# Folding the even rows of an fp32 sequence transform on the output side: matmuls of 189, 189 and 378 columns for three of 377

## Chip, cores, metric

One core of one Trainium2 chip; nothing else runs on it. The metric is the device time of one execution in microseconds, median of repeated runs.

## The reference

Shortened:

```python
batch, seq, dim = (8, 3008, 256)              # x
X = np.fft.fft(x, axis=1)                     # the sequence transform
X = np.fft.fft(X, axis=2)                     # the feature transform
attn = X.real
h = attn.reshape(B * S, D) @ w_in             # 24064 x 256 @ 256 x 2048
out = np.maximum(0.01 * h, h) @ w_out         # 2048 x 256
```

Everything is fp32. The kernel does the sequence transform as matmuls against cosine and sine tables, folds the feature transform into `w_in`, and uses a seven-product scheme for `w_out`.

## The kernel before

S = 3008, H = S/2, Q = S/4 = 752. Rows s and S-s, and rows s and H-s, are already added or subtracted on the input side, so that 377 even rows s = 2m (r = 0) and 376 odd ones (r = 1) remain, in three chunks of 128 partitions. A "unit" is one batch and one parity c of the output index k; a unit has two blocks (cosine, sine). The even sum and the odd sum of a block go to two PSUM banks, and their sum and difference are the outputs k and H+k.

```python
KW = [377, 376]                # columns of parity c

def m_order(r):
    m = np.arange(P)[:, None] + P * np.arange(NI)
    return np.where(m < (377, 376)[r], m, -1)

def dft_ps():                  # four banks, shared with cos_ps and sin_ps of up()
    return ps.tile([P, 512], F32, tag="up", bufs=4, name="dft_ps")

def sequence(ps_t, m, z_of, n, c):
    for i in range(NI):        # NI = 3                                  <- line 319
        nc.tensor.matmul(ps_t[0:m, 0 : KW[c]], lhsT=z_of(i), rhs=tabs[n, c][:, i, 0 : KW[c]],
                         start=(i == 0), stop=(i == NI - 1))

def butterfly(t, even_ps, odd_ps, m, c):
    kw, rest = KW[c], UW[c] - KW[c]
    ev = work.tile([P, KC], F32, tag="ev", bufs=2, name="ev")
    nc.scalar.copy(ev[0:m, 0:kw], even_ps[0:m, 0:kw])
    nc.vector.tensor_tensor(t[0:m, 0:kw], ev[0:m, 0:kw], odd_ps[0:m, 0:kw], op=ALU.add)
    nc.vector.tensor_tensor(t[0:m, kw : UW[c]], ev[0:m, 0:rest], odd_ps[0:m, 0:rest], op=ALU.subtract)
```

The rest of the program is a stream of steps. `up` makes hidden values from a finished unit (8 fp32 matmuls of 251 columns, line 386; VectorE adds the Nyquist term and forms g; ScalarE applies the leaky ReLU, line 397), `down` multiplies by `w_out` (7 matmuls of 251 columns, line 449, or 8 in the first two groups of 251 columns, line 429). The transforms of the next unit are emitted between the steps:

```python
def step(at):
    ...                        # up(j, f); three parts per unit, f = 0..7
    if f == 4:
        if part == 0: ...      # fold the rows of the next batch
        elif n > 0:
            dft(units[n + 1], part - 1)()
    ...                        # down of three steps ago

# the start, cut
convert(w0); fold_w_in(0, w0); convert(w2); fold_w_in(2 * WN, w2); spread_wn(0)()
fold_nyquist(); fold_rows(t0, 0); fold_rows(t0, 1); fold_halves(0, t0)
nyquist(0)()                   # the Nyquist column, 8 rows, by the same sequence()
dft(units[0], 0)(); spread(units[0]); dft(units[0], 1)()
o = load_w_out(0); convert(o); some_steps(2); ...
```

A compile-time list scheduler fixes the order of instructions on each engine ("the built order" below); the order in the source is not binding.

## Time and profile before

| | before |
|---|---|
| time, median of 3 | 1966.28 us |
| TensorE busy | 1945.9 us, 99% of the span |
| VectorE, GpSimd, ScalarE busy | 56%, 53%, 24% |
| waits of TensorE in all | 14 us, all before 40 us |

A matmul row of the profile reads: line, engine, operation, output <- inputs, shape, count | busy time, mean ns of one record | idle time before it. Because records overlap, the mean is a latency, not a cost; the cost is read from how far apart the records start. The lines themselves are in the prediction.

### The profile page before, as it was taken

What the parts mean: (1) busy time and instruction counts of PE and PEld (TensorE: products, weight loads), DVE (VectorE), ACT (ScalarE), POOL (GpSimd) and SP (SyncE); (2) the same over time, 40 slices, a digit from 0 to 9 for tenths busy, and PEclk for the clock granted to TensorE, in tenths of its full rate; (3) what the DMA queues carried; (4) which work ended last, traced back from release to release, by engine and by line L of the source; (5) the groups of instructions that cost most, each with busy time, mean ns of one, the idle gap of its engine ahead of it and who ended that gap; (6) DMA issues with size and microseconds to landing.
All of it is one profiled execution on the core that took longest, in us unless ns stands there. A gap on an engine that the chain in (4) does not pass through costs nothing.

```text
span 1964.4 us, 24292 instructions
## 1 busy us (share of the span) xinstructions
PE 1945.9 (99%) x8920; PEld 1687.8 (86%) x8920; DVE 1090.4 (56%) x2075; ACT 462.4 (24%) x526; POOL 1036.1 (53%) x1508
## 2 busy tenths in 40 slices
PE   7999999999999999999999999999999999999999
PEld 3788888888888888888888888888888888888888
DVE  8765455474545655466545654547545474545544
ACT  4422222222222222222222222222222222222221
POOL 0215555565555655556555665556645565555554
PEclk9999999999999999999999999999999999999999
DMA  8120000110001000020000200002000020000000
GB/s 314 41 86 19 11 19 22 35 60 11 19 22 75 19 11 30 11 81 13 22 19 11 83 22 11 19 11 83 22 11 19 11 94 11 16 14 22 11 11 22
DMA packets 25598, 70.99 MB, mean 36 GB/s; under 512 B 4596, under 2 KB 17268, under 8 KB 23432
## 3 DMA queue, kind: packets, MB, share of 16 engines
q1 hardware_dynamic: 23360, 69.43, 9.6%
q8 instruction: 71, 1.16, 0.3%
q14 instruction: 47, 0.39, 0.1%
q10 hardware_dynamic: 2120, 0.02, 0.1%
HBM read 44.72 MB, written 24.71 MB: 35 GB/s over the span
## 4 chain that ended last, share of the span: by engine, by line
PE 98%; DVE 1%; DMA 1%; ACT 0%; SPq 0%; issue 0%; DVEq 0%
PE sum_ps L449 56%; PE cos_ps L386 16%; PE sin_ps L386 16%; PE dft_ps L319 6%; PE sum_ps L429 3%; DMA raw<-in_w_in_dram 1%; PE up_ps L286 0%; DVE xt L189 0%; DVE power L262 0%; DVE win L263 0%; DVE xt L191 0%; DVE xt L200 0%; DVE xt L192 0%; DMA nyq_dram<-nyq 0%; ACT power L250 0%
## 5 line engine op out<-in xcount | busy, mean ns | idle before, releaser
L391 DVE SCALAR_TENSOR_TENSOR cos<-nb,wn,cos_ps 128x251 f32<-128x251 f32 (+1 forms) x768 | 330.6, 472 | 719.5 <-PE cos_ps L386 719.4
L397 ACT ACTIVATE g<-g 128x1004 f32<-128x1004 f32 (+1 forms) x384 | 399.1, 1039 | 1316.2 <-DVE g L396 1308.9
L404 POOL TENSOR_TENSOR s<-g 128x251 f32<-128x251 f32 (+1 forms) x368 | 271.7, 738 | 781.2 <-ACT g L397 781.2
L449 PE MATMUL sum_ps<-s,wt 128*128 128x251 f32 (+1 forms) x2208 | 527.6, 374 | 0.0
L449 PEld LDWEIGHTS sum_ps<-s,wt 128*128 128x128 f32 x2208 | 416.1, 188 | 52.6
L386 PE MATMUL sin_ps<-mix,wf 128*128 128x251 f32 (+1 forms) x1536 | 387.6, 374 | 0.8 <-DVE mix L327 0.8
L386 PE MATMUL cos_ps<-mix,wf 128*128 128x251 f32 (+1 forms) x1536 | 387.9, 374 | 0.0
L449 PE MATMUL sum_ps<-g,wo 128*128 128x251 f32 (+1 forms) x1472 | 372.5, 375 | 0.0
L386 PEld LDWEIGHTS cos_ps<-mix,wf 128*128 128x128 f32 x1536 | 291.2, 190 | 35.8 <-issue 1.0
L386 PEld LDWEIGHTS sin_ps<-mix,wf 128*128 128x128 f32 x1536 | 290.4, 189 | 35.7 <-DVE mix L327 1.2
L449 PEld LDWEIGHTS sum_ps<-g,wo 128*128 128x128 f32 x1472 | 279.6, 190 | 38.7
L395 DVE TENSOR_TENSOR g<-cos,sin_ps 128x502 f32<-128x502 f32 (+1 forms) x384 | 259.9, 677 | 49.9 <-DVE cos L391 9.3
L405 POOL TENSOR_TENSOR s<-s,g 128x251 f32<-128x251 f32 (+1 forms) x368 | 277.7, 755 | 0.0
L407 POOL TENSOR_TENSOR s<-g,s 128x251 f32<-128x251 f32 (+1 forms) x368 | 262.6, 714 | 28.6
L396 DVE TENSOR_TENSOR g<-cos,sin_ps 128x502 f32<-128x502 f32 (+1 forms) x384 | 257.2, 670 | 0.0
L406 POOL TENSOR_TENSOR s<-g 128x251 f32<-128x251 f32 (+1 forms) x368 | 241.6, 657 | 0.0
L449 PE MATMUL sum_ps<-g,wt 128*128 128x251 f32 (+1 forms) x736 | 215.8, 375 | 0.0
L449 PE MATMUL sum_ps<-s,wo 128*128 128x251 f32 (+1 forms) x736 | 215.8, 375 | 0.0
L449 PEld LDWEIGHTS sum_ps<-s,wo 128*128 128x128 f32 x736 | 139.5, 189 | 16.3
L449 PEld LDWEIGHTS sum_ps<-g,wt 128*128 128x128 f32 x736 | 139.8, 190 | 15.8
L319 PE MATMUL dft_ps<-tab,xt 128*128 128x377 f32 (+1 forms) x384 | 126.8, 479 | 1.0 <-DVE xt L199 1.0
L319 PEld LDWEIGHTS dft_ps<-tab,xt 128*128 128x128 f32 x384 | 72.7, 189 | 44.1 <-DVE xt L199 1.7
(46 smaller groups left out, 531.1 us busy)
## 6 DMA issues: line engine op xcount, KB each, us to landing
xt<-in_x_dram SPq DMA_DIRECT2D x16, 1536.0 KB, 9.6
out_dram<-o SPq DMA_DIRECT2D x80, 251.0 KB, 2.3
tab<-in_seq_tab_dram SPq DMA_DIRECT2D x8, 565.5 KB, 11.1
raw<-in_w_in_dram SPq DMA_DIRECT2D x8, 512.0 KB, 5.4
raw<-in_w_out_dram SPq DMA_DIRECT2D x8, 512.0 KB, 4.5
out_dram<-o SPq DMA_DIRECT2D x16, 250.0 KB, 2.4
nb<-nyq_dram SPq DMA_DIRECT2D x8, 376.5 KB
nb<-nyq_dram SPq DMA_DIRECT2D x8, 376.0 KB, 3.2
```

Source lines behind the costliest of these rows:

```text
L319: nc.tensor.matmul(ps_t[0:m, 0 : KW[c]], lhsT=z_of(i), rhs=tabs[n, c][:, i, 0 : KW[c]], start=(i == 0), stop=(i == NI - 1))
L386: nc.tensor.matmul(pt[blk][:, h * n : (h + 1) * n], lhsT=wf[:, blk, fs], rhs=mixed[b, c][blk][:, at : at + n], start=True, stop=True)
L391: nc.vector.scalar_tensor_tensor(cos[:, hs], in0=spreads[b, c][:, at : at + n], scalar=wn[:, h * NH + f : h * NH + f + 1], in1=pt[0][:, hs ...
L395: nc.vector.tensor_tensor(g[:, 0], cos[:, 0 : 2 * n], pt[1][:, 0 : 2 * n], op=ALU.add)
L396: nc.vector.tensor_tensor(g[:, 1], cos[:, 0 : 2 * n], pt[1][:, 0 : 2 * n], op=ALU.subtract)
L397: nc.scalar.activation(g, g, ACT.Lrelu)
L404: nc.gpsimd.tensor_tensor(s1, a[1][0], a[1][1], op=ALU.add)
L405: nc.gpsimd.tensor_tensor(s2, s1, a[0][0], op=ALU.subtract)
L406: nc.gpsimd.tensor_tensor(s3, a[0][0], a[1][0], op=ALU.subtract)
L407: nc.gpsimd.tensor_tensor(s4, a[0][1], s2, op=ALU.subtract)
L429: nc.tensor.matmul(sums[j][d][:, r * n : (r + 1) * n], lhsT=wo[:, h, f, d * P : (d + 1) * P], rhs=a[r][h], start=(f == 0 and r == 0 and h ...
L449: nc.tensor.matmul(sums[j][p], lhsT=still[p], rhs=moving[p], start=(f == 0 and i % 2 == 0), stop=(f == NH - 1), skip_group_check=True)
```

## The change

For s = 2m the angle at Q-k is a multiple of pi minus the one at k: with m even the cosine is the same and the sine changes sign, with m odd the other way round. So the sums over even m (E) and odd m (O) need only the lower half of the columns, and E+O is the output at k, E-O (sine: O-E) the one at Q-k. The rows are reordered so that chunk 0 holds even m, chunk 1 odd m, and chunk 2 half of each, with a table that is zero where the wrong rows are and twice as wide. The intent: 756 columns instead of 1131 for the even rows, paid for by two short VectorE operations. Below, a *sequence* is the set of six matmuls (12 records) that transforms one block or one Nyquist column; there are 34.

```diff
+KF = [189, 188]
+KP = [1, 0]
+TW = [4 * KF[0], NI * KC]
 def m_order(r):
-    m = np.arange(P)[:, None] + P * np.arange(NI)
-    return np.where(m < (377, 376)[r], m, -1)
+    at = np.arange(P)[:, None]
+    if r == 1: ...                            # as before
+    half = at // (P // 2)
+    m = np.concatenate([2 * at, 2 * at + 1, 2 * (P + at - half * (P // 2)) + half], axis=1)
+    return np.where(m < 377, m, -1)
+def k_order(c):
+    k = 2 * np.arange(KF[c])[::-1] + c
+    return np.concatenate([k, Q - k[KP[c] :]])
@@ seq_tables (cut)
+                parts = [t[:, 0], t[:, 1], t[:, 2] * (m[:, 2:] % 2 == 0), t[:, 2] * (m[:, 2:] % 2 == 1)]
@@ sequence
+        pe, po = dft_ps(), dft_ps()
+        for i, (lo, hi) in enumerate(((0, kf), (kf, 2 * kf), (0, 2 * kf))):
+            nc.tensor.matmul(pe[0:m, lo:hi], lhsT=z_of(i, 0), rhs=tab[:, i * kf : i * kf + hi - lo],
+                             start=(i == 0), stop=(i == NI - 1), skip_group_check=True)
         ...                                   # odd rows as before, into po
@@ butterfly
-        nc.scalar.copy(ev[0:m, 0:kw], even_ps[0:m, 0:kw])
+        nc.scalar.copy(e0[0:m, 0:kf], pe[0:m, 0:kf])
+        nc.vector.tensor_tensor(ev[0:m, 0:kf], e0[0:m, 0:kf], pe[0:m, kf : 2 * kf], op=ALU.add)
+        x, y = e0[0:m, KP[c] : kf], pe[0:m, kf + KP[c] : 2 * kf]
+        nc.vector.tensor_tensor(ev[0:m, kf:kw], *((x, y), (y, x))[part], op=ALU.subtract)
```

More of the change, by code (lines that the diff above doesn't have):

```diff
@@ L67, in m_order @@
 def m_order(r):
-    m = np.arange(P)[:, None] + P * np.arange(NI)
-    return np.where(m < (377, 376)[r], m, -1)
+    at = np.arange(P)[:, None]
+    if r == 1:
+        m = at + P * np.arange(NI)
+        return np.where(m < 376, m, -1)
+    half = at // (P // 2)
[4 more added lines that the diff above has]
+    return np.concatenate([k, Q - k[KP[c] :]])
 def laid_out(x):
@@ L91, in seq_tables @@
 def seq_tables():
-    out = np.zeros((4, 2, P, NI, KC), np.float32)
+    out = np.zeros((4, 2, P, TW[1]), np.float32)
     for r in range(2):
@@ L99, in seq_tables @@
         for c in range(2):
-            k = 2 * np.arange(KW[c]) + c
+            k = k_order(c)
             turn = (s[:, :, None] * k) % S
@@ L103, in seq_tables @@
             a = 2.0 * np.pi * turn / S
-            cos = np.where(4 * np.abs(turn) == S, 0.0, np.cos(a))
-            sin = np.where(np.abs(turn) == H, 0.0, np.sin(a))
-            out[r, c, :, :, : KW[c]] = weight[:, :, None] * cos
-            out[2 + r, c, :, :, : KW[c]] = weight[:, :, None] * sin
+            cos = weight[:, :, None] * np.where(4 * np.abs(turn) == S, 0.0, np.cos(a))
+            sin = weight[:, :, None] * np.where(np.abs(turn) == H, 0.0, np.sin(a))
+            for n, t in ((r, cos), (2 + r, sin)):
+                if r == 1:
+                    out[n, c].reshape(P, NI, KC)[:, :, : KW[c]] = t
+                    continue
+                kf = KF[c]
+                t = t[:, :, :kf]
+                parts = [t[:, 0], t[:, 1], t[:, 2] * (m[:, 2:] % 2 == 0), t[:, 2] * (m[:, 2:] % 2 == 1)]
+                out[n, c, :, : 4 * kf] = np.concatenate(parts, axis=1)
     return out
@@ L143, in columns @@
         half = col >= KW[c]
-        k = 2 * np.where(half, col - KW[c], col) + c
+        k = k_order(c)[np.where(half, col - KW[c], col)]
         plus, minus = np.where(half, H + k, k), np.where(half, H - k, (S - k) % S)
@@ L214, in load_tab @@
     def load_tab(q, n, c):
-        t = const.tile([P, NI, KC], F32, name=f"tab_{n}_{c}")
-        q.dma_start(t, seq_tab[n, c])
+        t = const.tile([P, TW[n % 2]], F32, name=f"tab_{n}_{c}")
+        q.dma_start(t, seq_tab[n, c, :, 0 : TW[n % 2]])
         tabs[n, c] = t
@@ L314, in combine_w_out, with sequence, butterfly @@
             nc.gpsimd.tensor_tensor(to, x, y, op=ALU.subtract)
-    def sequence(ps_t, m, z_of, n, c):
-        for i in range(NI):
-            nc.tensor.matmul(ps_t[0:m, 0 : KW[c]], lhsT=z_of(i), rhs=tabs[n, c][:, i, 0 : KW[c]],
-                             start=(i == 0), stop=(i == NI - 1))
-    def butterfly(t, even_ps, odd_ps, m, c):
-        kw, rest = KW[c], UW[c] - KW[c]
-        ev = work.tile([P, KC], F32, tag="ev", bufs=2, name="ev")
-        nc.scalar.copy(ev[0:m, 0:kw], even_ps[0:m, 0:kw])
-        nc.vector.tensor_tensor(t[0:m, 0:kw], ev[0:m, 0:kw], odd_ps[0:m, 0:kw], op=ALU.add)
-        nc.vector.tensor_tensor(t[0:m, kw : UW[c]], ev[0:m, 0:rest], odd_ps[0:m, 0:rest], op=ALU.subtract)
+    def sequence(z_of, m, part, c):
+        pe, po = dft_ps(), dft_ps()
+        kf, kw = KF[c], KW[c]
+        tab = tabs[2 * part, c]
+        for i, (lo, hi) in enumerate(((0, kf), (kf, 2 * kf), (0, 2 * kf))):
+            nc.tensor.matmul(pe[0:m, lo:hi], lhsT=z_of(i, 0), rhs=tab[:, i * kf : i * kf + hi - lo],
+                             start=(i == 0), stop=(i == NI - 1), skip_group_check=True)
+        tab = tabs[2 * part + 1, c].rearrange("p (i k) -> p i k", i=NI)
+        for i in range(NI):
+            nc.tensor.matmul(po[0:m, 0:kw], lhsT=z_of(i, 1), rhs=tab[:, i, 0:kw], start=(i == 0), stop=(i == NI - 1))
+        return pe, po
+    def butterfly(t, sums, m, part, c):
+        pe, po = sums
+        kf, kw, rest = KF[c], KW[c], UW[c] - KW[c]
+        e0 = work.tile([P, KF[0]], F32, tag="e0", bufs=2, name="e0")
+        ev = work.tile([P, KC], F32, tag="ev", bufs=2, name="ev")
+        nc.scalar.copy(e0[0:m, 0:kf], pe[0:m, 0:kf])
+        nc.vector.tensor_tensor(ev[0:m, 0:kf], e0[0:m, 0:kf], pe[0:m, kf : 2 * kf], op=ALU.add)
+        x, y = e0[0:m, KP[c] : kf], pe[0:m, kf + KP[c] : 2 * kf]
+        nc.vector.tensor_tensor(ev[0:m, kf:kw], *((x, y), (y, x))[part], op=ALU.subtract)
+        nc.vector.tensor_tensor(t[0:m, 0:kw], ev[0:m, 0:kw], po[0:m, 0:kw], op=ALU.add)
+        nc.vector.tensor_tensor(t[0:m, kw : UW[c]], ev[0:m, 0:rest], po[0:m, 0:rest], op=ALU.subtract)
     def dft(u, blk):
@@ L334, in dft @@
         z = zs[b]
-        pe, po = dft_ps(), dft_ps()
-        for r, pt in ((0, pe), (1, po)):
-            sequence(pt, P, lambda i: z[:, (c + blk) % 2, 2 * i + r, blk * P : (blk + 1) * P], 2 * blk + r, c)
+        sums = sequence(lambda i, r: z[:, (c + blk) % 2, 2 * i + r, blk * P : (blk + 1) * P], P, blk, c)
         def rest():
             t = work.tile([P, UW[0]], F32, tag=f"mix{blk}", bufs=2, name=f"mix{blk}")
-            butterfly(t, pe, po, P, c)
+            butterfly(t, sums, P, blk, c)
             mixed.setdefault(u, {})[blk] = t
@@ L354, in nyquist @@
     def nyquist(c):
-        pe, po = dft_ps(), dft_ps()
-        for r, pt in ((0, pe), (1, po)):
-            sequence(pt, B, lambda i: nya[:, c, i, r, :], r, c)
+        sums = sequence(lambda i, r: nya[:, c, i, r, :], B, 0, c)
         def rest():
             t = work.tile([P, UW[0]], F32, tag="mix0", bufs=2, name="nyq")
-            butterfly(t, pe, po, B, c)
+            butterfly(t, sums, B, 0, c)
             nc.sync.dma_start(nyq_dram[:, c, 0 : UW[c]], t[0:B, 0 : UW[c]])
```

## The prediction

> **What bounds the kernel now.** I read the page first: the busy times and the chain that ended last, then the two rows of the sequence transform.
>
> ```profile
> PE 1945.9 (99%) x8920; PEld 1687.8 (86%) x8920; DVE 1090.4 (56%) x2075; ACT 462.4 (24%) x526; POOL 1036.1 (53%) x1508
> ...
> PE 98%; DVE 1%; DMA 1%; ACT 0%; SPq 0%; issue 0%; DVEq 0%
> ...
> L319 PE MATMUL dft_ps<-tab,xt 128*128 128x377 f32 (+1 forms) x384 | 126.8, 479 | 1.0 <-DVE xt L199 1.0
> L319 PEld LDWEIGHTS dft_ps<-tab,xt 128*128 128x128 f32 x384 | 72.7, 189 | 44.1 <-DVE xt L199 1.7
> ```
>
> TensorE holds 98% of the chain; no other engine is over 56% busy. The transform (line 319) is 6% of the program. Its row counts 384 records for 192 matmuls of the program (16 units, 2 blocks, 2 row parities, 3 chunks): each fp32 matmul is two weight loads and two passes. Busy TensorE can hide short waits, because the records overlap (479 ns each, though they follow each other closer), so I read the waits of TensorE alone:
>
> ```profile
> PE up_ps L286 <- DVE win L263: 10.2, 1, 10.2
> PE sum_ps L429 <- ACT g L397: 2.0, 1, 2.0
> PE dft_ps L319 <- DVE xt L199: 1.0, 1, 1.0
> PE sin_ps L386 <- DVE mix L327: 0.8, 1, 0.8
> ```
>
> Four waits, 14 us, all before 40 us. From there to the last output TensorE never waits. So a nanosecond off its stream is a nanosecond off the time, except in the first 40 us, where VectorE (33.9 us busy of the first 40 in the view by stretches) sets the pace.
>
> The chain in order of time gives the real price of a matmul, since its pieces are the undisturbed stream:
>
> ```profile
> 124.32 3.40 PE sum_ps L429 x16
> ...
> 463.00 3.81 PE dft_ps L319 x12
> ...
> 582.43 3.79 PE dft_ps L319 x12
> ```
>
> 16 records of 251 columns take 3.40 us, 212.5 ns each; 12 of 377 take 3.81 us, 317.5 each; 12 of 376 take 3.79, 315.8 each. The slope is (317.5 - 212.5) / 126 = 0.833 ns per column and record, and 251 x 0.833 = 209 leaves some 3 ns of fixed cost. A column of a program matmul thus costs 1.67 ns, and splitting or keeping a matmul costs next to nothing.
>
> **What the Trainium skill says.** "FP8 and Floating Point Precision", TensorE Precision Notes: true fp32 takes four passes through the array. The trace agrees: two records at 2 cycles per column each (0.833 ns at 2.4 GHz). "TensorE: Matmul & The Clock Gate", Back-to-back issue gap: N/2.4 + 2.5 ns for a matmul by itself; with N counted twice for these records, 376 columns give 315.8 ns, as measured. The same section says that in a stream of load and matmul pairs a short matmul costs more (81 ns instead of 56 at 128 columns of bf16): a warning for the new short ones. Against it, on the same page, LDWEIGHTS: about P/1.2 ns, so 107 ns for 128 columns, while its record here is 189. No stream of the kernel before has a matmul short enough to decide this, but two cold starts show the load's true length. Four loads of line 386, usually 0.82 us from first start to last end, take 0.72 where the engine has no earlier weights to wait for:
>
> ```profile
> 79.07 0.72 PEld L386 LDWEIGHTS cos_ps<-mix,wf 128*128 128x128 f32 x4 [0.63 <-DVE power L262]
> 79.81 0.82 PEld L386 LDWEIGHTS sin_ps<-mix,wf 128*128 128x128 f32 x4
> ```
>
> In steady running each load starts with the matmul ahead of it, 212 ns apart. In the first group the second load came about 0.11 us after the first: the first matmul was streaming by then. So the array needs some 107 ns for a load, and the other 80 ns of the record are latency that overlaps.
>
> **The change part by part.**
>
> 1. *TensorE, removed.* Even rows: three matmuls of 377 (376) columns become 189, 189, 378 (188, 188, 376): 1131 - 756 = 375, and 1128 - 752 = 376 columns less. At 1.67 ns: 625 and 627 ns per sequence. The number of matmuls and weight loads is the same. There are 34 such sequences: 16 units x 2 blocks, and 2 for the Nyquist column. The piece of 3.80 us becomes 3.17.
>
> 2. *What of it is on the path.* Three sequences (Nyquist of c = 0, both blocks of the first unit) lie before 40 us, where TensorE waits for VectorE anyway: I count nothing for them. The other 31 (14 of c = 0, 17 of c = 1) stand in the gapless stream: 14 x 0.625 + 17 x 0.627 = 19.4 us.
>
> 3. *Weight loads behind short matmuls.* A record of 189 columns streams for 160 ns; the next load needs 107 by the reading above. It fits: nothing added.
>
> 4. *VectorE, added.* Two operations of 189 and 188 columns with one operand in PSUM per sequence. Same operation at 251 columns 408 ns (row of line 460), at 502 columns 677 (line 395): 1.07 ns per column and 139 fixed, so 341 ns each. 34 x 0.68 = 23 us more, 1090 to 1113, or 57% of the span. ScalarE's copy shrinks from 459 to some 320 ns (251 columns take 368).
>
> 5. *Whether that reaches TensorE.* The transform uses two of the four "up" banks, which TensorE wants again two steps later. One transform of the kernel before:
>
> ```profile
> 582.26 3.96 PE L319 MATMUL dft_ps<-tab,xt 128*128 128x376 f32 x12
> ...
> 584.94 0.45 ACT L326 COPY ev<-dft_ps 128x376 f32<-128x376 f32 x1
> ...
> 586.33 0.55 DVE L327 TENSOR_TENSOR mix<-ev,dft_ps 128x376 f32<-128x376 f32 x1 [2.45 <-PE dft_ps L319]
> 586.79 0.54 DVE L328 TENSOR_TENSOR mix<-ev,dft_ps 128x376 f32<-128x376 f32 x1
> ...
> 590.08 0.86 DVE L391 SCALAR_TENSOR_TENSOR cos<-nb,wn,cos_ps 128x251 f32<-128x251 f32 x2 [2.75 <-PE cos_ps L386]
> ```
>
> VectorE is done with the banks at 587.3 and then idles 2.75 us. The next step (589.03) uses the other two banks; these two are wanted at 589.03 + 4.67 (a step of 22 records of 212 ns) = 593.7. The margin is 6 us against 0.7 us of new work, and half of that can start earlier, because the even sum ends first. No wait. The two-deep mixing tiles are used three steps (14 us) later. TensorE's order after the start is otherwise the same (I compared the built instruction orders).
>
> 6. *The start.* Here the orders do differ. VectorE gets six new operations ahead of the first cos operation (two Nyquist, four for the two blocks), each advancing it by about 0.26 us (341 less the 80 ns by which neighbours overlap), 1.5 us, partly in its idle spots. The built order also puts only 4 instead of 10 sum matmuls ahead of the second batch of folded input weights, for which TensorE must wait for VectorE: up to 6 x 2 x 0.212 = 2.5 us of work moved behind a wait. On the other side the odd mixing tile comes earlier (the 0.8 us wait goes). I put the start at +2 us, an estimate with much room (0 to +4). A half-clock spell of 3.4 us (its records of 251 columns come every 419 ns from 39.3 to 42.6) follows the idle gap before it; it can come, move or go, which is 1.7 us either way.
>
> Sum: 1966.3 - 19.4 + 2.0 = **1948.9 us**, 0.9% less.
>
> **Rivals.**
>
> - *Short matmuls wait for their weights.* If the whole recorded load of 189 ns has to pass between matmul starts, each record of 189 columns costs 189 instead of 160. Four short records per sequence, 29 sequences with full weights on the path (the late Nyquist one has 8-column weights of 90 ns): 29 x 4 x 29 ns = 3.4 us given back, 1952. For it: the skill's dearer short matmuls. Against it: the cold starts.
> - *VectorE holds the banks.* If the longer evacuation were to stall TensorE by 0.6 us per transform, the gain would be gone: 1966. The margin of 6 us speaks against it; VectorE is at 56%. More likely is a small delay somewhere where the fold of the next batch's rows fills VectorE, but that fold lies in another step (part 0) than the transforms (parts 1 and 2).
> - *The start costs more or nothing.* With no loss and an idle half-clock spell gone, 1945; with both losses full, 1951.
> - *A gain over 2%* would need 39 us, twice all columns removed. Nothing here offers it.
> - Tables: two of four get smaller (756 of 1131 columns). They are on no chain now: the first transform waits for the folded rows, not for a table. No effect.
>
> **Range and chances.** The certain part is 19.4 us, with few tenths of doubt. The start gives -1 to +4 around it, the weight rival another +3.4 with perhaps one chance in four. That is 1945 to 1953. All of it lies within 2% (under 1926.9 would be needed for more), so that is nearly sure; what remains is left to a stall in every transform or a surprise in the build.
>
> **What would show it.** Right: the transform's pieces in the chain fall from 3.8 to 3.17 us; records of 189 columns start 160 ns apart (some 324 ns each as recorded, being 479 less 188 x 0.833); the number of TensorE records stays 8920 and the waits of TensorE stay in the first 60 us; VectorE's busy time rises by 23 us. The weight rival shows as pieces of about 3.29 us and short records 189 ns apart. The bank rival shows as a new wait of cos or sin (line 386's counterpart) for the mixing operations. A start that is worse shows as a later first sum matmul (39.3 now) and a new wait of the folded weights' matmul for VectorE. The prediction is wrong if a column removed from the stream does not return its 1.67 ns, or if the time from the first 60 us is off by more than 4.

## The result and the profile after

1949.36 us (1948.64 to 1949.78, 6 runs) against 1966.31 us (1964.49 to 1966.41, 6 runs): ratio 0.9916, interval 0.9903 to 0.9929. A ratio here is the mean of one kernel's fast runs over that of the other's of the same rounds, so it is not quite the ratio of the medians. Within 2%, 0.5 us from the predicted 1948.9.

Differences of 1 to 2 us need care. In the rounds of the experiments the 34 runs of the kernel before lie in two groups, 1964.4 to 1965.9 us (on average 1964.9; mean granted clock 1.000, in two runs 0.999) and 1966.0 to 1966.8 (on average 1966.4; 0.999). The averages are 1.5 us apart, near the 1.7 us that one half-clock spell of 3.4 us takes from a busy TensorE; start_unfolded below has the same two groups, at 1944.8 (1.000) and 1946.5 (0.999). Which group a median of the kernel before shows is chance: it goes from 1964.84 to 1966.31 between the rounds. The changed kernel has 0.998 in all ten of its runs, as with 6.8 us at half clock.

From the page of the changed kernel (line 354 is the odd rows, 350 the even rows, 364 the first added VectorE operation) and its groups by form:

```profile
PE 1924.5 (99%) x8920; PEld 1683.9 (86%) x8920; DVE 1109.9 (57%) x2143; ACT 458.9 (24%) x526; POOL 1039.1 (53%) x1508
```

```profile
L350 PE MATMUL dft_ps<-tab,xt 128*128 128x189 f32 x64 | 12.9, 324 | 1.8 <-issue 1.8
...
L350 PE MATMUL dft_ps<-tab,xt 128*128 128x378 f32 x32 | 12.8, 480 | 0.0
...
L364 DVE TENSOR_TENSOR ev<-e,dft_ps 128x189 f32<-128x189 f32 x16 | 5.6, 353 | 3.3 <-ACT e L363 3.3
...
L366 DVE TENSOR_TENSOR ev<-dft_ps,e 128x188 f32<-128x188 f32 x16 | 5.6, 348 | 0.0
...
L363 ACT COPY e<-dft_ps 128x189 f32<-128x189 f32 x16 | 5.1, 318 | 53.6 <-PE dft_ps L350 53.6
```

The number of TensorE records is the same, 8920. The short ones are recorded with 324 ns, as predicted. VectorE has 19.5 us more (23 predicted; the rows overlap by some 80 ns each, which the busy time counts once). In the chain in order of time, one transform is now two pieces:

```profile
579.55 1.27 PE dft_ps L350 x6
580.82 1.90 PE dft_ps L354 x6
```

1.27 + 1.90 = 3.17 us for 3.79. The starts of the short records in this transform are 158 to 159 ns apart, so no load of weights is waited for. Now the waits of TensorE:

```profile
PE up_ps L312 <- DVE win L289: 10.7, 1, 10.7
PE sum_ps L465 <- ACT g L433: 5.8, 1, 5.8
PE dft_ps L350 <- issue: 1.8, 1, 1.8
```

After the start there is still none. In the start, the wait before the first sum matmul has grown from 2.0 to 5.8 us. "issue" hides VectorE: its fold of the halves (line 225) ends at 25.4 in the order of time, and the transform starts at 25.48.

To see where the 17.1 us between the profiled spans come from, I matched the TensorE records of both traces by number (both have 8920, and from record 160 on the same order). At record 200, near 73 us, the changed kernel is 2.9 us *behind*; at the last record 17.1 us ahead. So 20.0 us were gained in the stream, and 2.9 us were lost before. The records of the 31 sequences themselves make up 19.4 of the 20.0: 0.627 us each, the predicted price. The other 0.6 us lie spread over the records between them, most of it in those of `sum_ps<-g,wo` (1392 of 251 columns, on average 212.46 ns apart for 212.96). The run before_lrelu below folds nothing and has 0.5 us of it all the same, so it does not need the removed columns; its cause stays open. The expectations below were written with 20.0/31 = 0.645 us per sequence, which is thus too much by 3%. The chain from 34 us on, before and after, shows the loss:

```profile
34.86 0.60 DVE wo L263
35.46 0.34 DVE win L248
35.80 1.16 DVE cos L391 x3
36.96 0.59 DVE g L395
37.55 0.60 DVE g L396
...
38.17 1.05 ACT g L397
...
39.26 6.20 PE sum_ps L429 x20
```

```profile
37.10 0.35 DVE power L275
...
37.47 0.73 ACT power L276
...
38.22 0.72 ACT power L277
...
38.96 1.28 ACT L433
...
40.26 1.05 ACT g L433
...
41.35 3.72 PE sum_ps L465 x8
```

VectorE reaches its first cos operation at 37.35 instead of 35.72. ScalarE's second table load (the piece "ACT L433" of 1.28 us), which lay beside other work before, now stands in front of the first activation. TensorE starts its sums 2.1 us later. "TensorE: Matmul & The Clock Gate", Part 1, says that after an idle window of some 3.4 us the clock is halved, and that the window runs freely. This trace agrees in the size: the half-clock spell is 3.4 us in the kernel before and 6.8 us in the changed one (5.8 us of idle ahead of it). It is seen in the granted clock (the number after the engines' busy times) of the stretch from 40 to 60 us, before and then after (0.93 of 20 us is 2.8 us at half clock, 0.84 is 6.4; the rest of each spell lies just before 40):

```profile
40.00:60.00 20.00, 20.00 (x72) 14.48 (x72) 18.39 (x39) 11.21 (x16) 0.00 (x0) 0.93 0.55 192
```

```profile
40.00:60.00 20.00, 18.65 (x60) 12.81 (x61) 18.70 (x39) 12.23 (x18) 0.20 (x1) 0.84 0.52 184
```

How much the clock takes differs between runs of one program. Four traces have the start of the changed kernel: after, hold6, hold20 and after_again. At the first sequence of the stream (record 212, at 75.2 us in the kernel before) they are 2.9, 1.7, 2.7 and 2.0 us behind. Half of TensorE's busy time inside the spell is what the clock took: 2.6, 1.8, 2.9 and 1.6 us, for 1.7 in the kernel before. TensorE's first record, which waits for the first weights, comes 0.5, 0.1, 0.0 and 0.5 us later. With both subtracted, all four are 1.6 us behind. So 1.6 us is the part of the loss that always comes back, near the 1.5 us that the prediction put on the six VectorE operations; the clock and the arrival of the weights add 0.1 to 1.4.

### The profile page after: what moved, and what is told of

Its sections match the earlier page's. It is cut to its first block, busy times and chain, and to the rows that moved or that the text cites. A ratio compares the mean times of both kernels' runs of the same rounds, so it can differ in the third digit from the quotient of the medians.

```text
span 1947.3 us, 24383 instructions
## 1 busy us (share of the span) xinstructions
PE 1924.5 (99%) x8920; PEld 1683.9 (86%) x8920; DVE 1109.9 (57%) x2143; ACT 458.9 (24%) x526; POOL 1039.1 (53%) x1508
## 4 chain that ended last, share of the span: by engine, by line
PE 98%; DVE 1%; DMA 0%; ACT 0%; issue 0%; SPq 0%; DVEq 0%; ACTq 0%
PE sum_ps L485 56%; PE cos_ps L422 17%; PE sin_ps L422 17%; PE dft_ps L354 3%; PE sum_ps L465 3%; PE dft_ps L350 2%; PE up_ps L312 1%; DMA raw<-in_w_in_dram 0%; DVE power L288 0%; DVE wo L289 0%; ACT L433 0%; DVE e L496 0%; DVE wo L287 0%; ACT g L433 0%; SPq L260 0%
## 5 line engine op out<-in xcount | busy, mean ns | idle before, releaser
L433 ACT ACTIVATE g<-g 128x1004 f32<-128x1004 f32 (+1 forms) x384 | 399.1, 1039 | 1208.3 <-DVE g L432 1199.9
L496 DVE TENSOR_TENSOR o<-e,sum_ps 128x251 f32<-128x251 f32 (+1 forms) x184 | 67.5, 409 | 8.7 <-ACT e L494 8.7
L354 PE MATMUL dft_ps<-tab,xt 128*128 128x377 f32 (+1 forms) x192 | 66.0, 479 | 0.0
```

Of the source, the lines that this page charges most:

```text
L354: nc.tensor.matmul(po[0:m, 0:kw], lhsT=z_of(i, 1), rhs=tab[:, i, 0:kw], start=(i == 0), stop=(i == NI - 1))
L433: nc.scalar.activation(g, g, ACT.Lrelu)
L496: nc.vector.tensor_tensor(to, x, y, op=ALU.add)
```

## The experiments

The main theory: every column taken from the gapless stream returns its 1.67 ns; the three sequences in the start return nothing, and their added VectorE operations cost there. Rivals: short matmuls pay for their weights; a longer evacuation of the banks is felt; the start's loss has another cause. All kernels below gave the right result.

### How short may a matmul be? (split_odd)

```diff
-            nc.tensor.matmul(po[0:m, 0:kw], lhsT=z_of(i, 1), rhs=tab[:, i, 0:kw], ...)
+            for j in range(4):
+                cs = slice(-(-kw * j // 4), -(-kw * (j + 1) // 4))
+                nc.tensor.matmul(po[0:m, cs], lhsT=z_of(i, 1), rhs=tab[:, i, cs], ...)
```

> The changed kernel with each odd-row matmul cut into four of 94 or 95 columns, result unchanged: 24 records of about 94 columns per sequence for 6 of 376 or 377. Theory (a record costs its columns, the true weight load is 107 ns and lies under the matmul ahead): a record streams for 81 ns, less than the load, so they come about 108 ns apart: 24 x 108 = 2.59 us for 1.90, +0.69 us x 31 = +21 us over the changed kernel, about 1971 us. Rival (the whole recorded load of 189 ns must pass): 24 x 189 = 4.54 us, +82 us, about 2031. Rival (columns alone): +1 us, about 1951.

1973.87 us (before 1964.84 in the same rounds; ratio 1.0047, interval 1.0031 to 1.0062). The changed kernel was not in these rounds, but hold6 below, which equals it, was 1948.65: 25.2 us less. The chain of this kernel:

```profile
585.94 1.27 PE dft_ps L350 x6
587.21 2.65 PE dft_ps L356 x24
```

The 24 records of 94 columns start 111 to 112 ns apart after a first step of 81, not all 81 (their columns) and not 190 (the recorded load). 2.65 us for 1.90 in 30 transforms give 22.5 us; TensorE's records show the same 22.5 for all 31 sequences against hold6, and the rest of the 25.2 lies outside of them (1.0 in the stream, 1.3 in the start). The 31st, the late Nyquist sequence, is a control: its weights have 8 columns, and there the same 94-column records start 80 to 85 ns apart. So with fresh 128-column fp32 weights before every record the floor is about 112 ns, it is the load that sets it and not the number of instructions, and a record of 189 columns (158 to 160 ns) is above it. The rival of the dear weight loads falls; the columns-only one too, for matmuls this short.

### Half the change (fold_blk0)

Block 1 keeps its three matmuls of 377 columns and its old combination; block 0 and the Nyquist column are folded.

```diff
+        if part == 1:
+            tab = tab.rearrange("p (i k) -> p i k", i=NI)
+            for i in range(NI):
+                nc.tensor.matmul(pe[0:m, 0:kw], lhsT=z_of(i, 0), rhs=tab[:, i, 0:kw], ...)
```

> The change for block 0 and the Nyquist column alone; block 1 (sines) as before. If the gain is columns: 7 x 0.625 + 9 x 0.627 = 10.0 us (10.3 at the 0.645 us per sequence that the two traces show) less a start that costs some two thirds of 2.5 us (4 of the 6 added VectorE operations): about 1957.7, 1956.5 to 1959. If the gain came from anything else than the number of folded sequences, it would not be about half.

1956.97 us (1956.36 to 1958.8; before 1964.84; ratio 0.996, interval 0.9948 to 0.9973): 7.9 us. The records of its sixteen folded sequences in the stream give 10.0 us in the trace, again 0.627 each: the stream part goes with the number of folded sequences. By the medians some 2.5 us were lost in the start, but this cannot be held against the whole change: the median of the kernel before is here one of the faster group, and the trace has a second half-clock spell (3.4 us at 25.5 us). With clock and arrival subtracted as above, its trace is 1.25 us behind at the first sequence of the stream, for 1.6 of the whole change (a rough figure: a later wait may hide part of what the early spell took).

### Holding the banks longer (hold6, hold20)

```diff
             mixed.setdefault(u, {})[blk] = t
+            if u[0] > 0:
+                d = work.tile([P, KC], F32, tag="d", bufs=1, name="d")
+                for _ in range(6):            # and 20
+                    nc.vector.tensor_tensor(d[:, 0 : KW[c]], t[:, 0 : KW[c]], sums[1][:, 0 : KW[c]], op=ALU.add)
```

> The changed kernel with 6 useless VectorE operations of 377 columns more per transform from the second batch on, each reading the odd sum's PSUM bank: 28 transforms x 6 x 0.46 us = 77 us more VectorE work, banks held 2.7 us longer. Theory (6 us of margin before TensorE wants the banks): no change, 1949.4 within 1 us. Rival (TensorE feels a longer evacuation): at least 0.5 us per transform, 1963 or more.

> The same with 20 useless operations: 9.1 us more per transform, over the margin of 6 us and, with the cos and g operations that lie between them, as long as three steps of TensorE. Theory: now TensorE waits, 1 to 3 us per transform, 28 to 84 us more, with new waits of cos or sin matmuls for VectorE in the profile. If it still shows nothing, the margin was misread.

hold6: 1948.65 us (4 runs), as the changed kernel. hold20: 1948.83 us (one look, state unknown), which is also the changed kernel's time. Its busy times, to be set against those of the changed kernel above:

```profile
PE 1925.1 (99%) x8920; PEld 1684.2 (86%) x8920; DVE 1362.9 (70%) x2703; ACT 458.9 (24%) x526; POOL 1026.2 (53%) x1508
```

VectorE does 253 us more and TensorE waits for none of it. So the rival falls further than I thought, and my expectation for 20 was wrong, and with it the reading of the margin: in the trace of hold20 the useless operations that read the odd bank of one transform run from 583.4 to 599 us, mixed with the cos and g operations of the following steps, and the cos and sin matmuls of 589.9 and 594.6 start without a wait. So the banks cannot be taken in strict turn, as I had assumed; the scheduler must have given those steps other ones (the profile does not name the banks). The margin is thus wider than the 6 us that I predicted; how wide, these runs do not say.

### The added VectorE work by itself (dve_alone)

In the kernel before, with no matmul changed:

```diff
         nc.scalar.copy(ev[0:m, 0:kw], even_ps[0:m, 0:kw])
+        nc.vector.tensor_tensor(d[0:m, 0 : kw - 188], ev[0:m, 0 : kw - 188], even_ps[0:m, 188:kw], op=ALU.add)
+        nc.vector.tensor_tensor(d[0:m, 189:377], ev[0:m, 0:188], even_ps[0:m, 0:188], op=ALU.subtract)
```

> The kernel before with only the added VectorE work of the change: two useless operations of 189 and 188 columns on the even sum's bank in every sequence, no matmul changed, result unchanged. Theory (the added operations cost only in the first 60 us, where VectorE paces TensorE): 1 to 4 us slower than before, all of it before 70 us, no new wait of TensorE after that. Rival (the start's loss of the change comes from the other instruction order or the tables, not from these operations): same as before within 0.5 us. Rival (they cost all along): 34 x 0.5 us, 15 us or more.

1969.34 us against 1965.52 (ratio 1.0019, interval 1.0006 to 1.0033): 3.8 us slower. TensorE's waits are three, all in the start, and the one before the first sum has become what it is in the changed kernel:

```profile
PE sum_ps L432 <- ACT g L400: 5.1, 1, 5.1
```

From record 212 to the last it takes 1884.4 us, as the kernel before does. The operations cost in the start alone, together with the order that the scheduler builds around them: the built order changes here in the same way (4 sum matmuls ahead of the second input weights). Which of the two it is this run cannot say.

### Attempts on the start that failed (before_lrelu, after_lrelu, after_pool)

First, one tiny leaky ReLU at the very start, so that its table is loaded once:

```diff
+    first = const.tile([P, 1], F32, name="first")
+    nc.scalar.activation(first, inf[:, 0:1], ACT.Lrelu)
```

> The kernel before with one tiny activation of the later function first, so that ScalarE's table is loaded once, at the start, and not a second time before the first activation of the hidden values. In the kernel before the second load (1.28 us at 32.8) is off the path, since the operation it delays waits until 38.1 for VectorE: expected no change, within 0.7 us.

> The same in the changed kernel. There the second load stands in the chain (38.96 to 40.25), but VectorE's g ends only at 39.77: expected the first sum matmul 0.5 us earlier (41.35 to about 40.85), the time 0.5 us less, if the order built stays the same. Rival (the table load is the whole of the start's loss): 1.3 to 2 us less.

before_lrelu: 1965.21 us against 1965.52, by the medians as expected. (Group by group it is 1.3 to 1.6 us faster, 1963.6 and 1965.2 against 1965.1 and 1966.6; 0.5 of this is in the stream.) after_lrelu: 1952.72 us (ratio 0.9934), some 3 to 4 us *slower* than the changed kernel. The chain shows the first cause; the pieces from the start of the wait on are:

```profile
18.68 5.38 DMA wn_dram<-wf
...
24.09 0.42 ACTq L324
...
25.10 0.32 ACT e L363
```

The scheduler put the issue of a DMA, which has to wait for another DMA, ahead of the Nyquist copy in ScalarE's queue. VectorE's combination of that copy stands ahead of the fold of the first unit's halves, in strict order, and so the first transform starts at 27.5 instead of 25.5. The first sum comes at 45.4. With the longer gaps TensorE also has two half-clock spells of 6.8 us, at 25.7 and 42.8 us. The run therefore tells nothing of the table load; it shows a chain that the change made: a Nyquist operation of VectorE ahead of the fold that TensorE waits for.

Second, the same combination moved to GpSimd for the first three sequences:

```diff
+        if early[0]:
+            e1 = work.tile([P, KF[0]], F32, tag="e1", bufs=2, name="e1")[0:m, 0:kf]
+            nc.scalar.copy(e1, pe[0:m, kf : 2 * kf])
+        v.tensor_tensor(ev[0:m, 0:kf], e0[0:m, 0:kf], e1, op=ALU.add)     # v = nc.gpsimd early, else nc.vector
```

> The changed kernel with the combination of the two even sums of the first three sequences (Nyquist and first unit) moved off VectorE: ScalarE copies both halves, GpSimd adds and subtracts. Six VectorE operations less in the start (1.5 us). If VectorE's extra work is what the start costs: 1 to 2.5 us less than the changed kernel, about 1947.5. But the built order also moves the sum matmuls further back behind the folded input weights (1 instead of 4 ahead of them), which may take up to 1.3 us of it back.

1953.64 us (ratio 0.9938), slower again: first sum at 46.7, since the built order now has one sum matmul ahead of the second input weights and more conversions ahead of the first cos; there are two half-clock spells again, 3.4 us at 25.9 and 6.8 us at 42.9. Whatever the removed operations are worth, the changed order took more; the run does not separate the two.

### Order set by hand (after_again, after_order, before_order)

```diff
-    convert(o)
-    some_steps(plain)
-    w = load_w_in(WN)
-    convert(w)
+    for part in o: part.begin()
+    some_steps(1)
+    with tc.issue_after(last_g[0].ins):       # VectorE's part of these after the first step's g
+        for part in o: part.end()
+        w = load_w_in(WN)
+        convert(w)
+    some_steps(plain - 1)
```

> The changed kernel itself once more, as the measure for the two reordered ones on the same chip: about 1949 us.

> The changed kernel with VectorE's order in the start set by hand: the first step's cos and g operations ahead of the conversion of the first output weights and of the second batch of input weights, so that ScalarE's table load and first activation (2.3 us) lie beside the conversion. The first sum matmul needs the weights, ready at about 39.9 instead of 41.35: 1 to 3 us less than the changed kernel (a shorter idle gap may also shorten the half-clock spell of 6.8 us), 1946 to 1948. If the start's loss has another cause than the order on VectorE: no change.

> The same reordering in the kernel before, whose built start order is then the same as the reordered changed kernel's. Between these two only the change itself differs: 31 sequences x 0.645 us = 20.0 less for the fold, plus six VectorE operations of 0.26 us (1.5 us) in the start: 18 to 19.5 us apart, where the unordered pair is 16.5 to 17 apart. If the difference stays at 17, the order was not what the start lost.

after_again 1948.40 us, after_order 1951.24, before_order 1969.96, with 1966.15 for the kernel before. The reordering made both kernels worse, by 2.8 and 3.8 us. The chain of after_order names a wait that I had not seen:

```profile
30.15 6.49 DMA nb<-nyq_dram
...
36.77 1.25 DVE cos L429 x3
```

The broadcast of the Nyquist row lands at 36.6. In the built orders VectorE converts weights until then; put in front, cos only waits. So my reading of the start ("cos could come earlier") was wrong. As a comparison the pair is still clean: with the same start order in both, the change is worth 1969.96 - 1951.24 = 18.7 us, within the 18 to 19.5 expected from 20.0 less 1.5 of VectorE. Without it the change is worth 17.0 to 17.7 by the medians. It would be tempting to read the difference as the share of the order, but the clock stands against it: both reordered kernels have a 6.8 us spell in their traces, while the plain pair compares 6.8 us with 3.4 or none. In the traces the reordered pair gains the same 20.0 us in the stream and loses 1.7 before it, and the plain pair loses 1.6 once clock and arrival are subtracted. So about 1.6 us go with the folding of the three sequences, and no further share of the order is shown, other than through the longer gap and the half-clock spell behind it.

### The first three sequences left unfolded (start_unfolded)

```diff
+        if early[0]:                          # Nyquist of c = 0 and the first unit: full table, as before
+            for i in range(NI):
+                nc.tensor.matmul(pe[0:m, 0:kw], lhsT=z_of(i, 0), rhs=full[:, i, 0:kw], ...)
+        else:
+            ...                               # folded; for c = 0 the masked third chunk is a tile of its own
@@ the start
     dft(units[0], 1)()
+    early[0] = False
```

> The change for all sequences but the first three (Nyquist of c = 0 and both blocks of the first unit), which stay unfolded, on their full tables; the start's built order is then the one of the kernel before, on every engine as far as the first sums. If the change's loss in the start (about 3 us in the traces) comes from folding those three, which stand where TensorE waits anyway: all of 31 x 0.645 us = 20.0 is left, about 1946.2 (1945.2 to 1947.2), the first sum matmul back at 39.3. If the loss has another cause (tables, the second column set): 1948 to 1949, as the changed kernel.

1945.72 us (1944.74 to 1946.53) against 1965.90: ratio 0.9897, interval 0.988 to 0.9913; 20.2 us (19.7 and 19.8 within the groups of equal clock), and 2.7 us below the changed kernel's 1948.40 in the rounds before. TensorE's waits are those of the kernel before, by number, place and nearly by size:

```profile
PE up_ps L324 <- DVE win L301: 10.4, 1, 10.4
PE sum_ps L487 <- ACT g L455: 2.0, 1, 2.0
PE dft_ps L363 <- DVE xt L229: 0.8, 1, 0.8
PE sin_ps L444 <- DVE mix L389: 0.8, 1, 0.8
```

The first sum is at 39.5 and the lag at record 200 is 0.2 us (the first weights came that much later). So folding these three sequences is the loss in the start, and not the tables or anything in the stream. This is the fastest version that I ran.

## Why the prediction was right

1. *1.67 ns per column.* Right: 3.79 to 3.17 us per transform, as predicted to the hundredth. The 31 sequences gave 19.44 us in TensorE's records, for 19.4. The stream as a whole gave 20.0; the other 0.6 us, most of which a kernel without the fold shows too, were not forecast.
2. *31 of 34 sequences on the path.* Right: leaving the first three out lost nothing and gave back the start (start_unfolded).
3. *Weights under short matmuls.* Right: 107 ns from two cold starts, against the recorded 189; split_odd measures 112 ns as the floor of a load and its record. (A slip in the sum of this rival: 30 sequences on the path have full weights, not 29, so it would have given back 3.5 us and not 3.4.)
4. *VectorE's added work.* Right in size (353 and 348 ns each for 341).
5. *No wait in the stream.* Right in result, but the reason was too narrow: the banks are not used in turn, and hold20 holds one for 15 us unnoticed.
6. *The start, +2 us.* 1.7 to 2.9 us in four traces of the same start: 1.6 us that always come back, and a clock that takes 1.6 to 2.9 us where it took 1.7. The 1.5 us for the six operations was right, and the half-clock spell was named as the uncertain part, "1.7 us either way". The 2.5 us for the changed order do not show by themselves, the new wait of the folded weights' matmul did not come, and the wait for the Nyquist broadcast was not foreseen. That the sum came so close (1948.9 for 1949.36) is in part luck: the unforeseen 0.6 us of the stream stand against the start's 0.9 too much in the profiled run. And the gain of 17 us is one against the slower group of the kernel before; against the faster it is 15.

## What to carry to other kernels

Where one engine runs without a gap, price a change by the slope between two shapes in the chain, not by the recorded means; and check each shorter matmul against the floor of its weight load. Apply a change only where the engine it relieves is the bound: here the same fold is a gain in the stream and a loss in the first 40 us. Under a list scheduler a small edit in a crowded start can move more time by reordering than by its own work, so compare pairs with the same built order, and look at the granted clock of each run before reading a difference of 1 to 2 us.

## What the Trainium skill lacked or had wrong

- "TensorE: Matmul & The Clock Gate", LDWEIGHTS: P/1.2 = 107 ns is what the array needs (two cold starts), but it does not say that the profile records 186 to 193 ns for it; whoever takes the record for the cost finds short matmuls far too dear.
- The same page, Back-to-back issue gap: its sustained figures (81 ns at 128 columns) are not given for fp32 and do not fit it. Here fp32 with new weights for every record runs at 111 to 112 ns per record of 94 columns (80 to 85 with weights of 8 columns), 158 to 159 at 188, 316 at 376: the larger of the columns at two cycles each and the load, and a few ns.
- "FP8 and Floating Point Precision", TensorE Precision Notes: the four passes of fp32 are right, but no page says that the profile shows them as two loads and two records per matmul (8920 records each of PE and PEld).
- The same TensorE page, Part 1: the clock is said to halve after an idle window of some 3.4 us. In the kernel before, a gap of 2.0 us (37.3 to 39.3), with a busy but broken stream ahead of it, was followed by 3.4 us at half clock; in the changed kernel a gap of 5.8 us by 6.8 us. The page gives no share of idle time that is enough; of the 3.4 us ahead of the first spell 58% were idle.
